# Gated feed-forward on one core: transposing a tile's activations by a DMA, with the down product one tile later

## The chip, the cores and the metric

The kernel runs on one core of a Trainium2 chip. The metric is device time in microseconds (us) of one execution; three executions of the kernel before took 1242.30, 1243.02 and 1243.65 us, so its time is the median, 1243.02 us.

## The reference

The program computes the output and all gradients (input, five weight matrices) of a four-layer stack on 2048 rows of width 512: linear attention with 32 heads, feed-forward, attention, feed-forward, with the same weights twice. Only the forward feed-forward matters here:

```python
def _B_ref(x, w_gate, w_up, w_down):          # F = 1376
    g = jnp.einsum("bsd,df->bsf", x, w_gate)
    u = jnp.einsum("bsd,df->bsf", x, w_up)
    h = _sigmoid(g) * u
    return jnp.einsum("bsf,fd->bsd", h, w_down)

x = x + _A_ref(_layernorm(x, axis=-1), A_wqkv, A_wo)
x = x + _B_ref(_layernorm(x, axis=-1), B_w_gate, B_w_up, B_w_down)
x = x + _A_ref(_layernorm(x, axis=-1), A_wqkv, A_wo)
x = x + _B_ref(_layernorm(x, axis=-1), B_w_gate, B_w_up, B_w_down)
```

## The kernel before, in words

The 2048 rows are 16 tiles of 128 rows (`NST`). The forward stretch of attention and feed-forward is one function, `ab_fwd`, called once for layers 0 and 1 and once for layers 2 and 3. One turn of its loop over `st` carries several tiles at once: the feed-forward of tile `st`, the end of attention of tile `st + 2` (`A.attn_y`, its product with `M` and the addition to the residual stream `xs`), the denominators and normalized queries of tile `st + 3` (`A.prod`, `A.front1`, `A.front2`, `A.front3`), the layer norm that feeds later tiles (`ln.apply`, `ln.stage_T`), and weight transposes for the backward pass (`fill`).

The order on TensorE, VectorE, ScalarE and GpSimd is the order of the program text: the whole forward part stands under a manual schedule for these four engines, and each works through its own instructions in that order. DMAs are issued from SyncE's queue, which is not among the four.

What one turn does for the feed-forward, with lines of the kernel:

- `gu(T, hT, fs)`, for the three slices `fs` of F (512, 512 and 352 columns): four products for the gate and four for the up projection on TensorE (L860), two sigmoids on ScalarE (L862, L864), the activation `hh = sigmoid(g) * u` on VectorE (L865) and `ssd`, kept for the backward pass, on GpSimd (L866).
- `transposes(T, fs)`: the down product needs `hh` with F on the partitions, so the 128x128 blocks of a slice (4, 4 and 3 of them) are transposed by TensorE into a PSUM bank (L874) and copied into the tile `hhT` by ScalarE (L877, L879).
- `finish(T)`: the down product, 11 products into one PSUM bank (L886), its addition to `xs` on VectorE (L888) and, in layer 1 where an attention layer follows, the layer-norm statistics of the new rows (`nxt.stats`: two instructions on VectorE, three on GpSimd).
- Three DMAs store `ssd` (L950) and `hh` (L951, L953) for the backward pass.

Beside these stand the front steps of attention. `front1` is a reduction on VectorE (L772). `front2` is three VectorE instructions (L782, L783, L784) whose last one writes the tile `pqnstage`. `front3` transposes that tile on TensorE (L330) and copies it out on ScalarE (L339).

So the text of a turn from the second slice on is, before: slice 1; transposes of slice 0; `stage_T`; `front1`; slice 2; `front2`; transposes of slice 1; `finish` of tile `st - 1`; `front3`; fill; transposes of slice 2; stores. `wide`, the pool of `ssd`, `hh` and `hhT`, has two buffers of each. The PSUM pool for `finish` and `attn_y` (`y`) has one bank, as has the one for `stage_T` and `front3` (`ln`).

Of the kernel before, what the change touches and what calls it, by code (L numbers as in the profile page):

```python
# [9 lines left out]
BF16 = mybir.dt.bfloat16  # L10
F32 = mybir.dt.float32
# [8 lines left out]
F = 1376  # L20
H = 32
DH = 16
P = 128
NST = S // P
NDC = D // P
NFC = (F + P - 1) // P
FLAST = F - (NFC - 1) * P
FSL = [(0, 512), (512, 512), (1024, F - 1024)]
EPS_LN = 1e-5
EPS = 1e-6  # L30
# [5 lines left out]
def fchunks_of_slice(fs):  # L36
    c0, w = FSL[fs]
    return list(range(c0 // P, (c0 + w + P - 1) // P))


def fc_rows(fc):
    return FLAST if fc == NFC - 1 else P

# [250 lines left out]
def build_consts(k, consts):  # L294
    nc = k.nc
    neghalf = consts.tile([P, 1], F32, name="neghalf")
    nc.gpsimd.memset(neghalf[:], -0.5)
    ident = consts.tile([P, P], BF16, name="ident")
    nc.gpsimd.memset(ident[:], 0.0)
    nc.gpsimd.affine_select(out=ident[:], in_=ident[:], compare_op=ALU.not_equal, fill=1.0,  # L300
                            base=0, pattern=[[-1, P]], channel_multiplier=1)
    bdmask = consts.tile([P, P], F32, name="bdmask")
    nc.gpsimd.memset(bdmask[:], 1.0)
    nc.gpsimd.affine_select(out=bdmask[:], in_=bdmask[:], compare_op=ALU.is_ge, fill=0.0,
                            base=0, pattern=[[-16, 8], [0, 16]], channel_multiplier=1)
    nc.gpsimd.affine_select(out=bdmask[:], in_=bdmask[:], compare_op=ALU.is_ge, fill=0.0,
                            base=15, pattern=[[16, 8], [0, 16]], channel_multiplier=-1)
    hsmask = consts.tile([P, 8], F32, name="hsmask")
    nc.gpsimd.memset(hsmask[:], 1.0)
    nc.gpsimd.affine_select(out=hsmask[:], in_=hsmask[:], compare_op=ALU.is_ge, fill=0.0,  # L310
                            base=0, pattern=[[-16, 8]], channel_multiplier=1)
    nc.gpsimd.affine_select(out=hsmask[:], in_=hsmask[:], compare_op=ALU.is_ge, fill=0.0,
                            base=15, pattern=[[16, 8]], channel_multiplier=-1)
    e0 = consts.tile([P, P], BF16, name="e0")
    nc.gpsimd.memset(e0[:], 0.0)
    nc.gpsimd.memset(e0[0:1, :], 1.0)
    k.e0 = e0
    k.tab = consts.tile([P, 1], F32, name="tab")
    k.neg = neghalf
    k.ones_sq = consts.tile([P, P], BF16, name="ones_sq")  # L320
    nc.gpsimd.memset(k.ones_sq[:], 1.0)
    k.ident, k.bdmask, k.hsmask, k.neghalf = ident, bdmask, hsmask, neghalf
# [520 lines left out]
def ab_fwd(k, A, ln, fill, nxt=None, out_cb=None, last_cb=None):  # L843
    nc, tc = k.nc, k.tc
    la, l = A.l, A.l + 1
    sva, sv = k.sv[la], k.sv[l]
    with ExitStack() as ctx:
        work = ctx.enter_context(tc.tile_pool(name=f"bf_work{l}", bufs=2, reuse_waits="tile"))
        wide = ctx.enter_context(tc.tile_pool(name=f"bf_wide{l}", bufs=2, reuse_waits="tile"))
        if out_cb is not None:  # L850
            k.ostg = ctx.enter_context(tc.tile_pool(name="out0_stg", bufs=2, reuse_waits="tile"))

        def gu(T, hT, fs):
            c0, w = FSL[fs]
            ssd_t, hh_t = T["ssd"], T["hh"]
            g_ps = ps_tile(k, "g", [P, 512], F32, "g_ps")
            u_ps = ps_tile(k, "u", [P, 512], F32, "u_ps")
            for ps, w_sb in ((g_ps, k.wg), (u_ps, k.wu)):
                for kc in range(NDC):
                    nc.tensor.matmul(ps[:, 0:w], lhsT=hT[:, kc, :], rhs=w_sb[:, kc, c0:c0 + w],  # L860
                                     start=(kc == 0), stop=(kc == NDC - 1))
            nc.scalar.activation(ssd_t[:, 0, c0:c0 + w], g_ps[:, 0:w], ACT.Sigmoid)  # L862
            oms = work.tile([P, 512], BF16, name="oms")
            nc.scalar.activation(oms[:, 0:w], g_ps[:, 0:w], ACT.Sigmoid, scale=-1.0)  # L864
            nc.vector.tensor_tensor(hh_t[:, c0:c0 + w], u_ps[:, 0:w], ssd_t[:, 0, c0:c0 + w], ALU.mult)  # L865
            nc.gpsimd.tensor_tensor(ssd_t[:, 1, c0:c0 + w], hh_t[:, c0:c0 + w], oms[:, 0:w], ALU.mult)  # L866

        def transposes(T, fs):
            hh_t, hhT = T["hh"], T["hhT"]
            fcs = fchunks_of_slice(fs)  # L870
            tps = ps_tile(k, "t", [P, 8, P], BF16, "t_tp")
            for i, fc in enumerate(fcs):
                r = fc_rows(fc)
                nc.tensor.transpose(tps[0:r, i, :], hh_t[:, fc * P:fc * P + r], k.ident[:])  # L874
            nfull = len([fc for fc in fcs if fc_rows(fc) == P])
            if nfull > 0:
                nc.scalar.copy(hhT[:, fcs[0]:fcs[0] + nfull, :], tps[:, 0:nfull, :])  # L877
            if nfull < len(fcs):
                nc.scalar.copy(hhT[0:FLAST, NFC - 1, :], tps[0:FLAST, nfull, :])  # L879

        def finish(T):
            st = T["st"]
            y_ps = ps_tile(k, "y", [P, D], F32, "y_ps")
            for fc in range(NFC):
                r = fc_rows(fc)
                nc.tensor.matmul(y_ps[:], lhsT=T["hhT"][0:r, fc, :], rhs=k.wd[0:r, fc, :],  # L886
                                 start=(fc == 0), stop=(fc == NFC - 1))
            nc.vector.tensor_tensor(k.xs[st][:], y_ps[:], k.xs[st][:], ALU.add)  # L888
            if nxt is not None:
                nxt.stats(st)  # L890

        def after(st):
            if st < 0:
                return
            if nxt is not None:
                nxt.apply(st)
            if out_cb is not None:
                out_cb(st)

        prev = None  # L900
        for st in range(NST):
            hT = ln.pop(st)
            T = dict(st=st,
                     ssd=wide.tile([P, 2, F], BF16, name="ssd_t"),
                     hh=wide.tile([P, F], BF16, name="hh_t"),
                     hhT=wide.tile([P, NFC, P], BF16, name="hhT"))
            nfill = fill.share(st)
            if st == 0:
                gu(T, hT, 0)
                A.extra("vector")  # L910
                A.front1(FLAG)
                A.front3(2)
                ln.apply(1)
                gu(T, hT, 1)
                transposes(T, 0)
                A.attn_y(2)
                ln.stage_T(1)
                gu(T, hT, 2)
                A.front2(FLAG)
            else:  # L920
                A.prod(st + FLAG)
                gu(T, hT, 0)
                A.attn_y(st + YLAG)
                after(st - 2)
                if nfill > 0:
                    fill("t", "vector")
                gu(T, hT, 1)
                transposes(T, 0)
                ln.stage_T(st + 1)
                A.front1(st + FLAG)  # L930
                gu(T, hT, 2)
                A.front2(st + FLAG)
            if l == 1 and st == NST - 1:
                nc.scalar.activation(k.tab[:], k.neg[:], ACT.Exp)
            transposes(T, 1)
            ln.apply(st + YLAG)
            if st == NST - 1:
                if last_cb is not None:
                    last_cb(0)
                if nxt is not None:  # L940
                    nxt.early_T()
            if st == 0:
                fill("t", "vector")
            if prev is not None:
                finish(prev)
            A.front3(st + FLAG)
            if st > 0 and nfill > 1:
                fill("t" * (nfill - 1), "scalar" if st % 2 else "vector")
            transposes(T, 2)
            nc.sync.dma_start(out=sv["ssd"][rows(st), :, :], in_=T["ssd"][:])  # L950
            nc.sync.dma_start(out=sv["hdd"][0, :, :, st, :].rearrange("g p w -> p g w"),  # L951
                              in_=T["hh"][:, 0:NG * GW].rearrange("p (g w) -> p g w", g=NG))
            nc.sync.dma_start(out=sv["hdl"][0, :, st, :], in_=T["hh"][:, NG * GW:F])  # L953
            prev = T
        if out_cb is not None:
            out_cb(NST - 2)
        if last_cb is not None:
            last_cb(1)
        finish(prev)
        if out_cb is not None:  # L960
            out_cb(NST - 1)

# [648 lines left out]
```

## Time and profile before

| what | value |
|---|---|
| median of three runs | 1243.02 us (1242.30 to 1243.65) |
| span of the profiled execution, first to last instruction | 1244.3 us |
| TensorE clock granted over the span | 0.986 of full |
| loop of `ab_fwd`, layer 1, from its first gate product to the next stage | 75.35 to 224.47 us |
| loop of `ab_fwd`, layer 3, from its first gate product to its last down product | 281.98 to 433.29 us |
| start of tiles 6, 7, 8, 9 of layer 1 (first gate product) | 131.41, 140.66, 149.84, 159.09 us |
| start of tiles 13, 14, 15 of layer 3 | 403.39, 412.56, 420.87 us |
| L874, the transposes of `hh` | 352 instructions, 219 ns each when seen alone |
| L877, L879, their copies on ScalarE | 64 of 586 ns, 32 of 379 ns, 32 of 273 ns |
| L886, the down product | 352 instructions, 379 ns each when seen alone |

The page gives no other time for the profiled execution than its span, which is 1.3 us above the median of the three runs. Products on TensorE overlap: a row of 379 ns is the time from the start to the modelled end of one, while in a run of them each starts 0.216 us after the one before (four in 0.865 us), and four transposes in a row take 0.22 us. A wait ("idle before") is put down to what ended it.

### The profile page before, as it was taken

How to read it: one execution, taken by the hardware profiler on the slowest of the kernel's cores; microseconds unless marked ns; L12 is line 12 of the kernel's file. 1: busy time of each engine (PE TensorE's matmuls, PEld its weight loads, DVE VectorE, ACT ScalarE, POOL GpSimd, SP SyncE). 2: the span in 40 equal slices, each digit the busy share in tenths (PEclk: the TensorE clock that was granted, in tenths of full speed). 3: DMA queues.
4: the chain of work that ended last, by engine and by line, in shares of the span. 5: the costliest groups of instructions: out<-in, count | busy, mean ns of one | idle time of the engine just before them, and what ended most of it. 6: DMA issues, size and time to landing. Idle time of an engine off the chain costs nothing. (4 is left out here: it accounts for less than half of the span.)

```text
span 1244.3 us, 22419 instructions
## 1 busy us (share of the span) xinstructions
PE 1197.8 (96%) x8646; PEld 720.2 (58%) x8646; DVE 726.8 (58%) x1410; ACT 600.7 (48%) x1105; POOL 258.1 (21%) x467
## 2 busy tenths in 40 slices
PE   8989999998999999998989999999999979999998
PEld 4445555455555555554745567755555745567777
DVE  6778886777777456664956620056664956642211
ACT  5677777557676644444626621144545616610001
POOL 4246765105665300000100010000000101200000
PEclk8999999999999999998999999999999989999999
DMA  7934455435536877858644488687767666579774
GB/s 234 300 111 166 167 182 175 167 118 182 198 137 212 280 231 240 265 168 287 227 130 144 126 287 287 175 281 216 215 201 236 172 213 182 162 245 335 238 195 147
DMA packets 266203, 256.08 MB, mean 206 GB/s; under 512 B 43248, under 2 KB 250992, under 8 KB 261232
## 3 DMA queue, kind: packets, MB, share of 16 engines
q1 hardware_dynamic: 266096, 254.65, 64.4%
q8 instruction: 67, 1.10, 0.4%
q14 instruction: 40, 0.33, 0.1%
HBM read 135.69 MB, written 118.92 MB: 205 GB/s over the span
## 5 line engine op out<-in xcount | busy, mean ns | idle before, releaser
L1309 PE MATMUL p_ps<-p_set,p_a 128*128 128x256 bf16 (+1 forms) x1792 | 186.3, 263 | 0.0
L1012 DVE TENSOR_TENSOR dd<-dhh_ps,ssd 128x512 bf16<-128x512 f32 x144 | 82.6, 629 | 157.1 <-PE dhh_ps L1004 150.6
L1309 PEld LDWEIGHTS <-p_a 128*128 128x128 bf16 x1792 | 159.0, 98 | 18.8
L1081 ACT COPY ddT<-T_ps 128x1024 bf16<-128x1024 bf16 (+1 forms) x96 | 82.9, 868 | 126.2 <-PE T_ps L1079 126.2
L866 POOL TENSOR_TENSOR ssd_t<-hh_t,oms 128x512 bf16<-128x512 bf16 (+1 forms) x96 | 101.6, 1064 | 55.0 <-ACT out_t L212 40.9
L1113 PEld LDWEIGHTS <-ddT 128*128 128x128 bf16 (+1 forms) x704 | 66.4, 98 | 70.1 <-issue 1.4
L860 PEld LDWEIGHTS <-hT 128*128 128x128 bf16 x768 | 71.6, 98 | 58.8 <-issue 1.7
L978 POOL TENSOR_SCALAR ab<-c 128x2 f32<-128x2 f32 x64 | 12.3, 192 | 448.8 <-DVE junk L975 437.5
L1288 DVE TENSOR_TENSOR dw_stg<-p_ps,dw_stg 128x512 bf16<-128x512 f32 (+2 forms) x43 | 28.3, 660 | 112.0 <-PE p_ps L1309 78.3
L860 PE MATMUL g_ps<-wg,hT 128*128 128x512 bf16 (+1 forms) x384 | 90.9, 359 | 1.2 <-DVE hT L337 1.2
L860 PE MATMUL u_ps<-wu,hT 128*128 128x512 bf16 (+1 forms) x384 | 90.9, 359 | 0.0
L865 DVE TENSOR_TENSOR hh_t<-u_ps,ssd_t 128x512 bf16<-128x512 f32 (+1 forms) x96 | 61.0, 636 | 48.3 <-PE u_ps L860 28.4
L1004 PE MATMUL dhh_ps<-wdT,gT 128*128 128x512 bf16 x372 | 83.8, 362 | 2.7 <-ACT gT L997 2.7
L1113 PE MATMUL dh_ps<-wgT,ddT 128*128 128x512 bf16 (+1 forms) x352 | 86.2, 379 | 0.0
L1113 PE MATMUL dh_ps<-wuT,ddT 128*128 128x512 bf16 (+1 forms) x352 | 81.3, 379 | 1.2 <-ACT t_sb L970 1.2
L886 PE MATMUL y_ps<-wd,hhT 128*128 128x512 bf16 (+1 forms) x352 | 81.3, 379 | 0.6 <-DVE x L888 0.6
L1297 PE MATMUL p_ps<-p_a,p_set 128*128 128x512 bf16 (+1 forms) x352 | 81.6, 383 | 0.0
L862 ACT ACTIVATE ssd_t<-g_ps 128x512 bf16<-128x512 f32 (+1 forms) x96 | 53.2, 554 | 32.8 <-PE g_ps L860 32.6
L975 DVE SCALAR_TENSOR_TENSOR junk<-t_sb,h_ld 128x512 bf16<-128x512 f32 x64 | 44.0, 687 | 39.8 <-ACT t_sb L970 39.8
L970 ACT ACTIVATE t_sb<-dh_ps,rstd_all 128x512 f32<-128x512 f32 x64 | 44.0, 687 | 38.1 <-issue 20.3
L1568 ACT CAST fin_o<-sg_ps 128x512 bf16<-128x512 f32 x4 | 2.3, 586 | 122.1 <-PE sg_ps L1566 122.1
L1290 ACT CAST dw_stg<-p_ps 128x512 bf16<-128x512 f32 (+2 forms) x43 | 24.0, 561 | 76.5 <-PE p_ps L1309 48.4
(226 smaller groups left out, 2224.2 us busy)
## 6 DMA issues: line engine op xcount, KB each, us to landing
p_set<-sv_hdd SPq DMA_DIRECT2D x30, 1024.0 KB, 6.4
sv_ssd<-ssd_t SPq DMA_DIRECT2D x32, 688.0 KB, 3.4
ssd<-sv_ssd SPq DMA_DIRECT2D x24, 688.0 KB, 5.0
sv_hdd<-dd SPq DMA_DIRECT2D x48, 320.0 KB, 3.5
sv_hdd<-hh_t SPq DMA_DIRECT2D x32, 320.0 KB, 2.6
h_ld<-sv_h SPq DMA_DIRECT2D x32, 256.0 KB, 4.4
p_set<-sv_dqk SPq DMA_DIRECT2D x8, 1024.0 KB, 5.8
p_a<-sv_h SPq DMA_DIRECT2D x12, 512.0 KB, 6.2
```

The costliest lines, as they stand in the source:

```text
L860: nc.tensor.matmul(ps[:, 0:w], lhsT=hT[:, kc, :], rhs=w_sb[:, kc, c0:c0 + w], start=(kc == 0), stop=(kc == NDC - 1))
L862: nc.scalar.activation(ssd_t[:, 0, c0:c0 + w], g_ps[:, 0:w], ACT.Sigmoid)
L865: nc.vector.tensor_tensor(hh_t[:, c0:c0 + w], u_ps[:, 0:w], ssd_t[:, 0, c0:c0 + w], ALU.mult)
L866: nc.gpsimd.tensor_tensor(ssd_t[:, 1, c0:c0 + w], hh_t[:, c0:c0 + w], oms[:, 0:w], ALU.mult)
L886: nc.tensor.matmul(y_ps[:], lhsT=T["hhT"][0:r, fc, :], rhs=k.wd[0:r, fc, :], start=(fc == 0), stop=(fc == NFC - 1))
L970: k.nc.scalar.activation(self.t[:], dh_ps, ACT.Identity, scale=rstd_col, accum_out=self.c12[:, 0:1])
L1004: k.nc.tensor.matmul(ps[:, 0:w], lhsT=gT[:, jc, :], rhs=k.wdT[:, jc, c0:c0 + w], start=(jc == 0), stop=(jc == NDC - 1))
L1012: k.nc.vector.tensor_tensor(dd[:, a, c0:c0 + w], ps[:, 0:w], ssd[:, a, c0:c0 + w], ALU.mult)
L1081: nc.scalar.copy(ddT[:, :, fcs[0]:fcs[0] + nfull, :], tps[:, :, 0:nfull, :])
L1113: nc.tensor.matmul(T["dh"][:], lhsT=T["ddT"][0:r, a, fc, :], rhs=(k.wuT, k.wgT)[a][0:r, fc, :], start=(i == 0), stop=(i == 2 * NFC - 1))
L1297: nc.tensor.matmul(ps[0:r, :], lhsT=set_t[:, st, j * P:j * P + r], rhs=g_all[:, st, :], start=(st == 0), stop=(st == NST - 1))
L1309: nc.tensor.matmul(ps[:, icl * w:(icl + 1) * w], lhsT=h_all[:, st, ic * P:(ic + 1) * P], rhs=set_t[:, st, 0:w], start=(st == 0), stop=(st ...
```

## The change

The 128x128 transposes of `hh` and their copies are taken out for all tiles but the last of each layer. A tile's `hh` is made 1408 columns wide, the last 32 set to zero on GpSimd at the start of the turn, and one DMA from SyncE's queue transposes it into `hhT`. `finish` of a tile moves from the end of the next turn to the middle of the turn after that, between the second slice and `stage_T`; the callback `after` (the layer norm of a finished tile, or the output copy) follows one tile later too. The last tile keeps its transposes on TensorE. The mask `bdmask` becomes bf16.

```diff
+        def dma_T(T):
+            T["hhT"] = wide.tile([P, NFC, P], BF16, name="hhT")
+            nc.sync.dma_start(out=T["hhT"][:], in_=T["hh"][:], transpose=True)
+
+        Ts = []
         for st in range(NST):
+            last = st == NST - 1
...
-                     hh=wide.tile([P, F], BF16, name="hh_t"),
-                     hhT=wide.tile([P, NFC, P], BF16, name="hhT"))
+                     hh=wide.tile([P, FP], BF16, name="hh_t"))
+            nc.gpsimd.memset(T["hh"][:, F:FP], 0.0)
+            Ts.append(T)
...
-                after(st - 2)
+                after(st - 3)
                 if nfill > 0:
                     fill("t", "vector")
                 gu(T, hT, 1)
-                transposes(T, 0)
+                if last:
+                    T["hhT"] = wide.tile([P, NFC, P], BF16, name="hhT")
+                    transposes(T, 0)
+                if st >= 2:
+                    finish(Ts[st - 2])
                 ln.stage_T(st + 1)
                 A.front1(st + FLAG)
                 gu(T, hT, 2)
                 A.front2(st + FLAG)
...
-            transposes(T, 1)
+            if last:
+                transposes(T, 1)
+            else:
+                dma_T(T)
             ln.apply(st + YLAG)
...
-            if prev is not None:
-                finish(prev)
+            if last:
+                finish(Ts[st - 1])
             A.front3(st + FLAG)
             if st > 0 and nfill > 1:
                 fill("t" * (nfill - 1), "scalar" if st % 2 else "vector")
-            transposes(T, 2)
+            if last:
+                transposes(T, 2)
...
-            prev = T
+        after(NST - 3)
...
-        finish(prev)
+        finish(T)
```

## The prediction

> **What bounds the kernel now.** I read the shares first, then the busy time of each engine in the two loops that the change touches, then one tile in order of time.
>
> ```profile
> PE 1197.8 (96%) x8646; PEld 720.2 (58%) x8646; DVE 726.8 (58%) x1410; ACT 600.7 (48%) x1105; POOL 258.1 (21%) x467
> 75.00:225.00 150.00, 146.98 (x963) 79.24 (x964) 116.97 (x221) 105.61 (x208) 94.47 (x150) 0.99 0.48 168
> 282.00:436.00 154.00, 152.07 (x1064) 85.88 (x1065) 107.14 (x205) 105.31 (x216) 86.41 (x109) 1.00 0.59 201
> ```
>
> TensorE is busy 96% of the span, and 98 to 99% in both loops (rows two and three: window, its length, then PE, PEld, DVE, ACT, POOL). VectorE is next: 117 of 150 us in layer 1. The average says "take work off TensorE". One tile of layer 1 in order of time says where that is dangerous:
>
> ```profile
> 146.24 0.76 PE L860 MATMUL u_ps<-wu,hT 128*128 128x352 bf16 x4
> 146.84 0.39 PE L874 MATMUL t_tp<-ident,hh_t 128*128 128x128 bf16 x4
> 147.06 2.54 PE L886 MATMUL y_ps<-wd,hhT 128*128 128x512 bf16 x11
> 147.11 0.52 DVE L865 TENSOR_TENSOR hh_t<-u_ps,ssd_t 128x352 bf16<-128x352 f32 x1
> 147.55 0.51 DVE L782 TENSOR_SCALAR den<-den 128x32 f32<-128x32 f32 x1
> 148.10 0.35 DVE L783 RECIPROCAL rden_all<-den 128x32 f32<-128x32 f32 x1
> 148.49 0.90 DVE L784 TENSOR_TENSOR pqnstage<-pq_all,rden_all 128x512 bf16<-128x512 bf16 x1
> 149.44 0.23 PEld L330 LDWEIGHTS <-pqnstage 128*128 128x128 bf16 x4 [0.33 <-DVE pqnstage L784]
> 149.64 0.69 DVE L888 TENSOR_TENSOR x<-y_ps,x 128x512 f32<-128x512 f32 x1 [0.25 <-PE y_ps L886]
> ```
>
> Slice 2 ends on TensorE at 146.84. Only then can VectorE do the last `hh` and the three instructions of `front2`, and their result is there at 149.4. TensorE needs it for `front3` at 149.44. The 2.6 us between are filled by the transposes of slice 1 and the down product: it arrives just in time, with a weight-load wait of 0.33 us. Tile 0 has no down product in that place, and shows what then happens:
>
> ```profile
> 82.63 0.76 PE L860 MATMUL u_ps<-wu,hT 128*128 128x352 bf16 x4
> 83.22 0.39 PE L874 MATMUL t_tp<-ident,hh_t 128*128 128x128 bf16 x4
> 83.45 0.39 PE L365 MATMUL wT_ps<-ident,wqkv 128*128 128x128 bf16 x4
> 85.64 0.40 PE L330 MATMUL ln_tp<-ident,pqnstage 128*128 128x128 bf16 x4 [1.81 <-DVE pqnstage L784]
> ```
>
> **What is taken away.** 30 tiles lose 4 + 4 + 3 transposes: 0.22 + 0.22 + 0.17 = 0.61 us of TensorE each, 18.3 us in all. ScalarE loses 0.59 + 0.59 + 0.38 + 0.27 = 1.83 us a tile; with 106 of 150 us busy it sets nothing, so I count 0.
>
> **What moves.** The down product leaves the place between slice 2 and `front3` and goes ahead of slice 2. Its VectorE work (the addition, in layer 1 the statistics too) now stands ahead of the `hT` copy, `front1`, the last `hh` and `front2`. TensorE reaches `front3` early, VectorE late. The steps of a middle tile of layer 1, from its first gate product (140.66 before):
>
> - TensorE: slice 0 1.73, `attn_y` 0.87, a fill 0.22, slice 1 1.73: the down product starts at 4.54 (before, the transposes of slice 0 at 145.20). It takes 2.38, then `stage_T` 0.22 and slice 2 1.19: free at 8.33.
> - VectorE: the addition starts 2.58 after the first down product (137.81 to 140.39), so at 7.12. From there the spacings of the rows: statistics +0.72, aggregate +0.73, `hT` copy +0.10, `front1` +0.33, last `hh` +0.70, L782 +0.44, L783 +0.55, L784 +0.39, and TensorE loads it 0.95 later: 4.91 in all, at 12.03.
> - `front3` takes 0.22, and the next tile starts at 12.25. Before it took 9.18 to 9.25.
>
> TensorE idles 8.33 to 12.03 = 3.7 us a tile where it lost 0.61 us of work. VectorE in turn idles from its last `front2` to the next slice 0, about 2 us, so nothing catches up. Tiles 2 to 12 have both a moved down product and a `front3`: seven with a fill gain 3.03, four without a fill (12.03 against a mean of 9.10) gain 2.93: **+32.9 us**. Tiles 13 and 14 have no `front3`, but the next gate product waits for the `hT` copy behind the statistics: +0.25 each. Tiles 0 and 1 have no moved down product: -0.4 each. The last tile has one down product more: +2.4. Layer 1: **+35.0**.
>
> Layer 3 has no statistics after the addition: the copy follows it by 0.61 (384.18 to 384.79), L782 takes 0.20, L784 is read 1.09 after its start: 7.12 + 0.61 + 0.33 + 0.70 + 0.44 + 0.20 + 0.38 + 1.09 = 10.87, then `front3` and a fill 0.44: 11.32 against 9.40. 11 x 1.92 = **+21.1**; tiles 13 and 14 gain the 0.6, tiles 0 and 1 0.4 each, the last tile costs 2.4: **+21.5**.
>
> **What is added.** The zeroing on GpSimd (128 x 32) lies between the 0.22 us of L426 and the 0.85 us of 352 columns of L866; I take 0.25. GpSimd is busy 94 of 150 us, and what VectorE needs of it (`prod`, 1.16 us) starts a tile early; cost 0, and 32 x 0.25 = 8 us without that cover. The bf16 mask serves four VectorE instructions: 0, and at most 4 x 0.69 us either way.
>
> No row of before shows a DMA that transposes. From below: the store of `hh` (320 KB, same source) lands in 2.6 us. From above: the page's 266203 packets took 64.4% of 16 x 1244.3 us, 48 ns each; 1408 rows of 256 B would be 4.2 us, pieces of 32 B 34 us. I take 6 us, near the first. SyncE waits for the last `hh` (done at 10.2) before it; queued behind are the three stores, which nobody reads in this loop but whose end frees the two buffers. The down product reads `hhT` at 4.54 two turns on, 18.8 us after 10.2; the buffer of `hh` is zeroed again two turns on, 14.3 us after 10.2, less 3.4 for the stores: up to 10.9 us the transpose costs nothing.
>
> The Trainium skill ("Advanced Engine Details and Errata", X-Bar Transpose) says that such a DMA is as fast as an ordinary one, 350 to 400 GB/s; by that 360 KB take about 1 us (an estimate), and the sum stays as it is. No run shown here has one.
>
> **The clock.** After long stretches with transposes or nothing on TensorE, the granted clock drops:
>
> ```profile
> 75.35 1.88 PE L860 MATMUL g_ps<-wg,hT 128*128 128x512 bf16 x4 [0.57 <-DVE hT L337]
> 75.30:79.00 3.70, 3.65 (x13) 1.43 (x14) 1.46 (x3) 1.82 (x4) 1.06 (x3) 0.54 0.49 172
> ```
>
> From 71.82 to 75.35 there was no product but transposes; then two groups of four took 1.67 and 1.70 us in place of 0.87, 1.65 us lost. Of five such gaps of 2.8 to 3.5 us in this trace (71.82, 83.22, 278.51, 288.17, 648.37) the first and last were followed by slow products. The change makes 11 gaps of 3.9 us (8.33 to 12.25) and 11 of 3.0. I let half of the first and a quarter of the second be hit: 8 x 1.65 = **+13 us**; none is 0, all 36.
>
> The Trainium skill ("TensorE: Matmul & The Clock Gate", Part 1) says that an idle window of about 3.4 us halves the clock; the 0.54 agrees. By that rule alone the 3.0 us gaps are never hit, and the gap from 648.37, 2.8 us, disagrees.
>
> **Sum.** 35.0 + 21.5 + 13 = 69.5 us. On the span that is 1313.8, less the 1.3 us by which the span exceeds the median: **1312 us**, 5.6% more.
>
> **Rivals.**
> - The clock falls in every one of the 22 gaps: 56.5 + 36 = +93, 1336 us. For it: a gap of 2.8 us sufficed once. Against: three gaps did not. [...] Chance 0.20.
> - The transpose takes longer than some 11 us and the buffers of `hh` hold the turn: at 20 us each pair of turns is 9 us longer, 26 x 4.6 = +120 or more, 1430 us. For it: no row excludes small pieces. Against: nothing in the trace says that they are small. Chance 0.13.
> - Faster: `pqnstage` is there when TensorE has ended slice 2, so that only the 18.3 us of removed transposes count: 1225 us. It needs VectorE's chain to end by 8.33 in place of 12.03. Tile 0 speaks against it: there TensorE waited 1.81 us with two groups of transposes in between and no addition ahead. Chance 0.05.
> - Both cancel (within 0.2%, about what a measurement of this kernel can tell): the wait would have to be 0.6 us. Chance 0.02.
>
> The forecast's own case holds 0.60: without any slow clock 1299, with less contention on VectorE (L782 took 0.17 to 0.57) some 10 less, and chain spacings off by 0.5 us a tile are 11 more or less. The range is 1280 to 1365: it holds the forecast and the clock rival, and leaves out the slow transpose and the two other signs. Slower 0.93, same 0.02, faster 0.05.
>
> **What would show it.** L330 on `pqnstage` with some 2.5 to 3.7 us of waiting on VectorE L784 in tiles 2 to 12; tile starts 12.2 us apart in layer 1 and 11.3 in layer 3; L874 with 22 instructions; granted clock under 0.95 in both loops. Wrong would be: tile starts 8.6 us apart (no wait), or waits for the transposing DMA at L886, L865 or the zeroing (the second rival).

## The result

The changed kernel takes 1323.06 us (three runs, 1319.05 to 1323.42) against 1243.02: a ratio of 1.0626, 95% interval 1.0595 to 1.0657. The profiled execution spans 1321.0 us. The page's engine shares, and below them the two loops of `ab_fwd` (window, its length, then PE, PEld, DVE, ACT and POOL busy, granted clock, DMA share, GB/s):

```profile
PE 1212.0 (92%) x8316; PEld 708.2 (54%) x8316; DVE 720.5 (55%) x1410; ACT 551.3 (42%) x985; POOL 264.3 (20%) x499
74.70:273.40 198.70, 157.27 (x795) 74.26 (x794) 111.31 (x219) 79.93 (x146) 100.42 (x166) 0.90 0.51 153
331.00:515.50 184.50, 155.18 (x867) 77.06 (x868) 104.35 (x202) 79.66 (x153) 86.17 (x124) 0.93 0.63 191
```

TensorE has 330 instructions fewer and is busy 79% and 84% of the loops, not 98 to 99%; and it is slower where it works, at a clock of 0.90 and 0.93. The loop of layer 1, from its first gate product to the next stage, took 149.1 us (75.35 to 224.47) and takes 198.9 (74.50 to 273.43), 50 us more. That of layer 3, to its last down product, took 151.3 us (281.98 to 433.29) and takes 184.9 (330.97 to 515.84), 34 us more. The spans differ by 77 us only, since the rest of the program, on which the change has hardly any bearing, was some 7 us shorter in the execution profiled here. One tile of layer 1 in order of time, TensorE and VectorE:

```profile
165.09 2.54 PE L887 MATMUL y_ps<-wd,hhT 128*128 128x512 bf16 x11
167.67 0.69 DVE L889 TENSOR_TENSOR x<-y_ps,x 128x512 f32<-128x512 f32 x1 [1.62 <-PE y_ps L887]
168.29 0.76 PE L861 MATMUL u_ps<-wu,hT 128*128 128x352 bf16 x4
168.39 0.69 DVE L424 BATCH_NORM_STATS2 ln_stats<-x 128x6 f32<-128x512 f32 x1
169.12 0.18 DVE L426 BATCH_NORM_AGGREGATE ln_mv<-ln_stats 128x2 f32<-128x6 f32 x1
169.22 0.39 DVE L338 COPY hT<-ln_tp 128x512 bf16<-128x512 bf16 x1
169.53 0.68 DVE L773 TENSOR_REDUCE den<-prod 128x32 f32<-128x512 bf16 x1
170.12 0.51 DVE L866 TENSOR_TENSOR hh_t<-u_ps,ssd_t 128x352 bf16<-128x352 f32 x1
170.55 0.17 DVE L783 TENSOR_SCALAR den<-den 128x32 f32<-128x32 f32 x1
170.75 0.35 DVE L784 RECIPROCAL rden_all<-den 128x32 f32<-128x32 f32 x1
171.14 1.04 DVE L785 TENSOR_TENSOR pqnstage<-pq_all,rden_all 128x512 bf16<-128x512 bf16 x1
172.24 0.40 PE L331 MATMUL ln_tp<-ident,pqnstage 128*128 128x128 bf16 x4 [3.19 <-DVE pqnstage L785]
172.47 1.74 PE L861 MATMUL g_ps<-wg,hT 128*128 128x512 bf16 x4
174.00 1.91 PE L861 MATMUL u_ps<-wu,hT 128*128 128x512 bf16 x4
175.71 1.20 PE L806 MATMUL y_ps<-M_sb,pqnT 128*128 128x512 bf16 x4
176.97 1.03 PE L861 MATMUL g_ps<-wg,hT 128*128 128x512 bf16 x4
```

Read it from the addition (L889) on: VectorE is never idle until `pqnstage` is written at 172.2, while TensorE ended slice 2 at 169.05 (168.29 + 0.76) and waits 3.19 us. Then four gate products take 1.53 us and four up products 1.71, where 0.87 was the rule before: the clock is at half until about 176, some 3.4 us. The waits over each loop, layer 1 first (us in total, times, the longest; TensorE's weight loads and its transposes side by side, which are one wait, not two):

```profile
PEld L331 <- DVE pqnstage L785: 44.0, 13, 3.5
PE ln_tp L331 <- DVE pqnstage L785: 39.6, 13, 3.2
PEld L331 <- DVE pqnstage L785: 33.8, 13, 2.7
PE ln_tp L331 <- DVE pqnstage L785: 29.3, 13, 2.3
```

The transposing DMA itself is cheap. Its rows (line, queue, count, the time that it holds SyncE's queue in ns, first and last start) and its time to landing:

```profile
L903 SPq DMA_TRANSPOSE hhT<-hh_t x30: 1263/1392/2184, 81.8 to 501.7; - x30
DMA to landing us min/median/max: 3.5/3.5/4.4
```

### The profile page after: what moved, and what is told of

Read it like the earlier page. It is cut to its first block, busy times and chain, and to the rows that moved or that the text cites. A ratio compares the mean times of both kernels' runs of the same rounds, so it can differ in the third digit from the quotient of the medians.

```text
span 1321.0 us, 21708 instructions
## 1 busy us (share of the span) xinstructions
PE 1212.0 (92%) x8316; PEld 708.2 (54%) x8316; DVE 720.5 (55%) x1410; ACT 551.3 (42%) x985; POOL 264.3 (20%) x499
## 5 line engine op out<-in xcount | busy, mean ns | idle before, releaser
L861 PEld LDWEIGHTS <-hT 128*128 128x128 bf16 x768 | 76.5, 105 | 74.7 <-issue 25.9
L861 PE MATMUL u_ps<-wu,hT 128*128 128x512 bf16 (+1 forms) x384 | 107.1, 408 | 0.0
L861 PE MATMUL g_ps<-wg,hT 128*128 128x512 bf16 (+1 forms) x384 | 100.6, 389 | 2.4 <-DVE hT L338 2.4
L887 PE MATMUL y_ps<-wd,hhT 128*128 128x512 bf16 (+1 forms) x352 | 81.3, 379 | 0.6 <-DVE x L889 0.6
L331 PE MATMUL ln_tp<-ident,pqnstage 128*128 128x128 bf16 x128 | 12.9, 224 | 69.7 <-DVE pqnstage L785 69.7
L887 PEld LDWEIGHTS <-hhT 128*128 128x128 bf16 (+1 forms) x352 | 34.2, 98 | 41.1 <-issue 0.7
```

## The experiments

The theory: the loss is the place of the down product. It left the gap between slice 2 and `front3`, and put its addition ahead of `front2` on VectorE; TensorE now waits for `pqnstage`, and the long gaps lower its clock. The rival: the transposing DMA costs the time, through its queue, its traffic or its latency. Ratios are to the kernel before, run on the same chip.

**down_back.** The changed kernel with the down product behind slice 2 again, still two turns back.

```diff
-                if st >= 2:
+                if last:
                     finish(Ts[st - 2])
...
             if last:
                 finish(Ts[st - 1])
+            elif st >= 2:
+                finish(Ts[st - 2])
             A.front3(st + FLAG)
```

> The changed kernel with one thing put back: the down product (still of the tile two turns back, still fed by the transposing DMA) stands again between slice 2 and front3; only the last tile keeps its place. Theory (the loss is the place of the down product: front3 waits for pqnstage, and the long gap lowers the clock): the wait at L331 falls under 0.5 us a tile, the clock goes back to 0.99, and with 18 us of transposes gone and one down product more at the end of each layer the time is 1228 to 1237 us. Rival (the transposing DMA itself, its queue or its traffic, costs the time): it stays above 1290 us.

Measured: 1238.5 us (ratio 0.9964, 0.9937 to 0.9991), 1.5 us above the range that the theory gave. Some 85 us went with one move, the DMAs all in place: TensorE waits for `pqnstage` 7.7 us in all in layer 1, in place of 39.6, and the granted clock is 0.98 and 0.99 in the two loops.

**dma_only.** The kernel before, with the DMA in place of the transposes and nothing moved.

```diff
...
-            transposes(T, 1)
+            if st == NST - 1:
+                transposes(T, 1)
+            else:
+                nc.sync.dma_start(out=T["hhT"][:], in_=T["hh"][:], transpose=True)
...
```

> The kernel before with one thing done alone: the transposes of all tiles but the last go to the DMA (with the zeroing and the bf16 mask); the down product stays where it was, one turn behind. Theory: 18 us of transposes go, some 0.2 us a tile of that comes back as waiting on pqnstage, since one group of four transposes no longer lies in front of front3: 1226 to 1234 us. The DMA is issued some 8 us before the down product reads it, against 3.5 us to landing, so no wait for it. Rival (the DMA costs the time): above 1290 us, or waits for the DMA at the down product.

Measured: 1232.42 us (ratio 0.9898, 0.9867 to 0.9928), as the theory had it: the part of the change that was meant to be its core is a gain of 11 us. A tile of layer 1 in it:

```profile
143.18 0.76 PE L861 MATMUL u_ps<-wu,hT 128*128 128x352 bf16 x4
143.77 2.54 PE L887 MATMUL y_ps<-wd,hhT 128*128 128x512 bf16 x11
144.73 1.37 SPq L940 DMA_TRANSPOSE hhT<-hh_t  x1
146.55 0.40 PE L331 MATMUL ln_tp<-ident,pqnstage 128*128 128x128 bf16 x4 [0.24 <-DVE pqnstage L785]
152.74 2.54 PE L887 MATMUL y_ps<-wd,hhT 128*128 128x512 bf16 x11
```

The DMA of 144.73 is read at 152.74, 8.0 us later, and lands after 3.5: the down product need not come a tile later for it. TensorE waits 0.24 us for `pqnstage`, and a turn with a fill takes 8.97 us in place of 9.2 (one without a fill took 8.96 before).

**move_only.** The changed kernel with the transposes on TensorE for every tile.

```diff
+                T["hhT"] = wide.tile([P, NFC, P], BF16, name="hhT")
+                transposes(T, 0)
...
-            if last:
-                transposes(T, 1)
-            else:
-                dma_T(T)
+            transposes(T, 1)
```

> The changed kernel with the transposes left on TensorE for all tiles, the down product two turns back and ahead of slice 2 as in the changed kernel. Theory: the chain slice 1, down product, addition, pqnstage, front3 is the same, and the transposes of slice 1 fall into its gap: 1310 to 1335 us. Rival (the DMA costs the time): about the time before, 1240 to 1255 us.

Measured: 1340.53 us (ratio 1.0768, 1.0714 to 1.0822). No DMA transposes at all, and it is slower than the changed kernel, by 17 us, about the 18.3 us of transposes. It lies 5 us above the range, but the rival is out: the move alone makes the whole loss.

**gap_products.** The changed kernel with products that nobody reads ahead of `front3`.

```diff
+            if 0 < st < NST - FLAG:
+                kps = ps_tile(k, "t", [P, 512], F32, "keep_ps")
+                for i in range(12 if l == 1 else 9):
+                    nc.tensor.matmul(kps[:], lhsT=k.ident[:], rhs=k.wg[:, 0, 0:512], start=True, stop=True)
             A.front3(st + FLAG)
```

> The changed kernel with products added that nobody reads: ahead of front3 of tiles 1 to 12, twelve (layer 1) or nine (layer 3) products of 128x512, some 2.6 and 1.9 us, which fit into the wait for pqnstage. Theory (the part of the loss beyond the wait is the clock, which falls after gaps without products): granted clock 0.99 in both loops, no slow gate products, 1288 to 1298 us. Rival (the clock is no cause): 1318 us or more.

Measured: 1293.64 us (ratio 1.0387, 1.0335 to 1.0439). More work on TensorE, and 29 us less than the changed kernel. Both loops, clock in the third column from the right:

```profile
75.00:260.00 185.00, 173.19 (x956) 86.08 (x972) 117.12 (x232) 83.53 (x153) 101.33 (x169) 1.00 0.56 167
310.00:490.00 180.00, 172.26 (x1011) 88.54 (x1029) 109.09 (x211) 83.39 (x159) 86.88 (x125) 0.99 0.69 208
```

So the 80 us are 29 of clock and 51 of the rest, the wait above all.

**gap_transposes.** The same with 46 and 34 transposes in place of the products.

> As gap_products, but what is added ahead of front3 is transposes of 128x128 that nobody reads: 46 (layer 1) or 34 (layer 3), some 2.5 and 1.9 us. One theory: only products keep the clock up, transposes do not count: the clock falls as in the changed kernel, 1315 to 1328 us. The rival: any work on TensorE keeps it up: 0.99 in both loops and 1288 to 1298 us.

Measured: 1296.17 us (ratio 1.0434, 1.0399 to 1.0468). The rival here is right: transposes that fill the gaps keep the clock up as products do.

```profile
75.00:260.00 185.00, 172.42 (x1358) 103.23 (x1372) 115.69 (x229) 82.68 (x152) 101.44 (x169) 0.99 0.57 167
310.00:490.00 180.00, 170.93 (x1327) 102.12 (x1343) 111.56 (x219) 86.38 (x164) 87.93 (x128) 1.00 0.70 208
```

**gap_few.** As gap_products, three products in either layer (`range(3)`).

> As gap_products with only three products (0.65 us) at the start of the gap; behind them TensorE stays idle for 2.5 us in layer 1 and 1.6 us in layer 3, and from the last product to the next gate product it is 3.3 and 2.4 us. Theory A (the clock falls only after a whole idle window of about 3.4 us): never, 1288 to 1299 us. Theory B (what counts is the share of a window in which TensorE works): still some slow turns in layer 1, 1300 to 1318 us.

Measured: 1312.51 us (ratio 1.0563, 1.0525 to 1.0601).

```profile
75.00:265.00 190.00, 156.14 (x776) 73.89 (x790) 107.35 (x211) 75.69 (x139) 97.57 (x159) 0.90 0.51 151
310.00:505.00 195.00, 170.37 (x1037) 89.04 (x1056) 119.98 (x234) 93.61 (x177) 89.18 (x129) 0.99 0.65 196
```

Layer 3 is back at 0.99, layer 1 is as slow as without them. In a turn of layer 1 there TensorE ends the added products at 140.8, is idle for 2.54 us, makes the four transposes of `front3` and takes up its gate products at 143.57: less than 3 us without a product, and still the next four up products take 1.7 us (144.69 to 146.39). Theory A is out; theory B fits.

**front_early.** The changed kernel with `front2` made before the addition.

```diff
+                ln.stage_T(st + 1)
+                A.front1(st + FLAG)
+                A.front2(st + FLAG)
                 if st >= 2:
                     finish(Ts[st - 2])
-                ln.stage_T(st + 1)
-                A.front1(st + FLAG)
                 gu(T, hT, 2)
-                A.front2(st + FLAG)
```

> The changed kernel with stage_T, front1 and front2 ahead of the down product, so that VectorE makes pqnstage before the addition and the last slice; the down product stays ahead of slice 2 and two turns back. Theory (only the order on VectorE made front3 late): no wait at L331 in tiles 2 to 12, TensorE sets the turn at 8.6 to 8.8 us, less 18 us of transposes, plus one down product more at the end of each layer: 1226 to 1238 us. Rival (the place of the down product on TensorE itself, or its delay by two turns, costs): above 1260 us.

Measured: 1232.46 us (ratio 0.9915, 0.9884 to 0.9947). The down product stands where the change put it, one tile later, and nothing is lost: what made `front3` late is the order on VectorE. The turns with a fill take 9.0 us in layer 1, though, somewhat over the 8.6 to 8.8 expected: TensorE still waits 0.27 us for `pqnstage` in them, where the theory had no wait.

**down_back_two.** down_back with each transposing DMA issued twice, one after the other, into the same tile.

> The kernel down_back with each transposing DMA issued twice into the same tile, the second after the first has landed. Theory (the DMA is hidden, with 18 us between the last slice and the down product): the same as down_back within 4 us, 1235 to 1242 us. Rival (SyncE's queue or the traffic costs something): 30 x 1.4 us of SyncE or more on top, above 1250 us.

Measured: 1264.34 us (ratio 1.0183, 1.0158 to 1.0208). The expectation failed: the DMA was not hidden when doubled, it cost 26 us. Who waited for an instruction that writes or reads `hhT`, over the whole run (us, times):

```profile
  POOL hh_t L913: 33.4, 12
  DVE x L889: 24.7, 9
  PEld L887: 5.9, 2
DMA to landing us min/median/max: 3.5/4.8/8.3
```

The down product (L887) waits little for the DMA; the 24.7 us of the addition (L889) are waits for the down product itself (16.3 in down_back). What waits for the DMAs is the zeroing of the next `hh` (L913): the buffer of `hh` is free only when the DMAs that read it are done. It waits 19.3 us more for a store of `hh`, which stands behind the doubled DMAs in SyncE's queue, so the queue that the rival named has a part in the loss; how the 26 us divide between buffer and queue is not shown. In down_back the first DMA has to wait as well, until the down product two turns back has read the buffer that it writes, and so it starts later than it could (in one turn of down_back at 148.04, where the last `hh` was done at 146.33); a turn is 9 us. I had counted the 18 us to the down product as the cover and not the shorter one of the buffer.

**two_transposes.** The same doubling in the changed kernel.

> The changed kernel with each transposing DMA issued twice into the same tile, the second after the first has landed (3.5 us to landing each). Theory (in the changed kernel the DMA is issued right after the last slice, and the buffer of hh is wanted some 14 us later): the doubled DMA is still hidden, 1315 to 1328 us, no waits at the zeroing. Rival (as in down_back_two, where the doubling cost 26 us): above 1340 us.

Measured: 1326.15 us (ratio 1.0673, 1.0630 to 1.0717), 3 us over the changed kernel, with overlapping intervals. There the DMA starts as soon as the last slice is there and the turn is 11.2 to 13.6 us long; the zeroing waits twice in the whole run, 5.3 us in all, and both times for a store, not for a transposing DMA. This is the cover of 14.3 us in the prediction, and two DMAs stay within it.

**dma_front_early.** dma_only with `front2` ahead of slice 2.

```diff
                 ln.stage_T(st + 1)
                 A.front1(st + FLAG)
-                gu(T, hT, 2)
                 A.front2(st + FLAG)
+                gu(T, hT, 2)
```

> The kernel dma_only with front2 ahead of slice 2 on VectorE. In dma_only a tile of layer 1 still waits 0.24 us for pqnstage. Theory: that wait goes, 11 tiles in layer 1 gain some 0.25 us and tiles 0 and 1 of both layers up to 2 us each: 1222 to 1229 us. Rival (VectorE as a whole is the bound there): no change from dma_only, 1229 to 1234 us.

Measured: 1226.32 us (ratio 0.9868, 0.9842 to 0.9894), the fastest of all: it beats both kernels. The turn in layer 1 is 8.58 us, in a profiled execution that was itself the shortest of the five (1214.60 us).

**order_only.** The kernel before with that same edit, without any DMA transposes.

> The kernel before with front2 moved ahead of slice 2 and nothing else. Theory (the order on VectorE is worth something by itself only where TensorE waits for pqnstage, 0.33 us of weight loads in some tiles of layer 1 and 1.8 us in tile 0 of each layer): 1236 to 1242 us. Rival (the order does all of what dma_front_early gained, the DMA nothing): 1224 to 1229 us.

Measured: 1243.49 us (ratio 1.0007, 0.9988 to 1.0026): nothing, neither the small gain of the theory nor that of the rival. In before, VectorE was in time by itself; only with 0.6 us less on TensorE does the order matter.

## Why the prediction was right, and where its sizes were off

The forecast was 1312 us, the time is 1323. That the two lie so close is in part luck: the wait was put some 5 us too high and the clock some 16 too low, and these partly cancel.

- **The wait** was the right mechanism, and its chain holds step by step: addition 2.58 us after the first down product (165.09 to 167.67), then the order of VectorE down to `pqnstage`. The chain took 4.57 us from the addition to `front3` against 4.91: the step from L782 to L783 (L783 to L784 in the changed kernel) took 0.20, not the 0.55 that before showed in layer 1. With the clock held, in gap_products, turns of layer 1 take 11.93 us with a fill and 11.70 without (12.25 and 12.03 forecast), those of layer 3 11.22 (11.32). The term of +56.5 came out as +51.
- **The clock** is the term that was mis-sized: +13 forecast, 29 measured. The step that failed is "half of the first and a quarter of the second be hit". Of the 11 long gaps 10 were hit and of the 11 short ones 6. Four more low stretches follow the gaps of tiles 0 and 1 of both layers, which the sum did not count. That makes 20 in place of 8, at 1.5 to 1.7 us each some 34 us; gap_products, which keeps one such stretch in layer 3, gave 29 back. The price of 1.65 us was right. The count came from five gaps in the trace of before as if they were draws. Nor were they all: that trace has three more, behind the loops, with 2.71 to 2.89 us of idle time each, and every one went with a granted clock of 0.50 (from 631.77, 809.26 and 1003.82). Of the 22 gaps of the rival "all 22", 16 were hit, so the truth lies nearer the rival than the forecast.
- **The clock rule.** The Trainium skill ("TensorE: Matmul & The Clock Gate", Part 1) has the clock halved after an idle window of about 3.4 us, and its Part 4 says that transposes do not engage the full clock. That the low clock lasts some 3.4 us and doubles the time of a product, the trace agrees. The rest differs: in gap_few stretches of less than 3 us without a product were enough, and in gap_transposes transposes held 0.99. The measurements decide.
- **The other terms.** Tile 14 of layer 1 takes 8.26 us against 8.08 (+0.25 forecast), the last tile 13.85 against 11.49 (+2.4 forecast). The zeroing takes 0.12 us on GpSimd (0.25 taken); it and the mask cost nothing that shows.
- **The DMA** lands in 3.5 us; 6 were taken, 4.2 worked out for rows of 256 B. The profile page of the changed kernel counts 43200 packets more, 1440 for each DMA of 352 KB, so the pieces are of about 250 B and the rival with small pieces is out. The 320 KB store of `hh` takes 2.6 us in before and 4.2 in the changed kernel, where it stands behind the transposing DMA. That a transposing DMA is as fast as another, which the Trainium skill ("Advanced Engine Details and Errata", X-Bar Transpose) states, these times bear out roughly; the 1 us estimated from its bandwidth they do not.
- **The gain** that the change was after is real, and 0.6 us a tile was the right measure for it: move_only differs from the changed kernel by 17 us. In dma_only 11 of the 18 us remain; 0.24 us a tile in layer 1 went to the same wait, and dma_front_early takes 6 of them back.

**What decides which gap is hit** can be read from the trace of the changed kernel. Its low stretches last 3.41 us and begin a whole number of such steps apart, as if on a fixed grid: those from 145.31, 158.96 and 172.61 us are four steps apart. Two gaps of 3.19 us each, cut along that grid (window, its length, TensorE busy, granted clock, DMA share, GB/s):

```profile
114.58:117.99 3.41, 2.18 (x16) 1.00 0.00 0
117.99:121.41 3.42, 1.46 (x10) 1.00 0.60 126
169.20:172.61 3.41, 0.37 (x5) 1.00 0.22 43
172.61:176.02 3.41, 3.41 (x10) 0.50 1.04 323
```

The first gap (116.76 to 119.95) falls across a grid line, and the clock stays at full speed; the second (169.05 to 172.24) lies nearly whole in one step, and the next step runs at half clock. Of the 112 steps at full clock between 70 and 520 us, the 20 in which TensorE was busy for a share of 0.40 or less were followed by a low clock, and the 92 with a share of 0.42 or more were not; in gap_few the two sides are 0.38 and 0.45. So a turn of 13.61 us, nearly four steps (13.65), brings its gap to the same place of the grid each time and is hit from tile 6 to tile 12 without exception, and in layer 3, where turns of 11.2 and 12.9 us alternate, two turns of 24.1 us are nearly seven steps (23.9).

What stays open: the exact share of work from which the clock falls, and how transposes count in it. Other traces have single steps that fall otherwise: in before, the step from 72.18 to 75.59, busy for a share of 0.52 and mostly with transposes, was followed by a low clock. Stretches of products and of transposes of several lengths would have to be varied one by one for that.

## What to carry to other kernels

When work is taken off the engine that is busy all the time, ask what its busy time was hiding: here 2.4 us of products covered a chain of VectorE that has the same length, and moving them exposed the chain although the engine had less to do. Where an operation moves on one engine, its followers on the others move too; write the order of the second engine down as well, and time the chain to the next operation that the first one needs. A transfer's cover ends not only where its result is read but also where its source buffer is wanted again.

## What the runs showed of the hardware that was not expected

A TensorE that is busy with transposes of 128x128 keeps its granted clock (0.99 and 1.00 with 46 or 34 of them in each gap). A gap of less than 3 us without products, 0.65 us of products just ahead of it, was enough to halve the clock for some 3.4 us in turn after turn. In the changed kernel the clock fell and rose only on a grid of 3.41 us, and in the two loops it fell just where TensorE had been busy for a share of 0.40 or less of the step before. Added work that nobody reads made the kernel 29 us faster.
